# Partial results of the expert products: a running sum for product 7 alone, sum S1 on VectorE, scaling on ScalarE, and an in-SBUF finish in the last expert

## The chip, the cores and the metric

One core of one Trainium2 chip runs the whole program in one launch. The metric is the device time of that core in microseconds (us), the median of several executions. Of the core's engines TensorE (PE in the rows, its weight loads PEld) multiplies matrices, VectorE (DVE) and ScalarE (ACT) do elementwise work and are the ones that read the matmul results in PSUM, GpSimd (POOL) does elementwise work on SBUF and issues the transfers that add while they move data, and SyncE (SP) issues plain transfers.

## The reference

Attention with bucketed keys, then one gated block (`a * b @ w3 @ w_out`), then four experts. The change lies in the four experts only:

```python
def _moe2_ref(x, domain_probs, w1, w2):          # x [1536, 512], w1 [4, 512, 1024], w2 [4, 1024, 512]
    p = domain_probs / (domain_probs.sum(-1, keepdims=True) + 1e-09)
    out = np.zeros((N, D), dtype=np.float32)
    for e in range(E):                            # E = 4
        h = np.maximum(x @ w1[e], 0.0)
        out += p[:, e:e + 1] * (h @ w2[e])
    return out
```

## The kernel before

All matrices are float32. A float32 operand is split into a high part (rounded to the fast matmul type, done by ScalarE) and a low part (the rest, done by VectorE), and each product is three matmuls: high-high, high-low, low-high. Every operand of TensorE therefore needs one ScalarE and one VectorE instruction first.

**The two stages of an expert.** Both products of an expert use Strassen's scheme in Winograd's form: seven half-size products P1 to P7 in place of eight. The first stage (`fp_products`) makes the hidden activations, kept in eight pairs of SBUF rows (`kept`). The second stage multiplies them with `w2`. It runs the products in the order P1, P4, P6, P7, P5, P2, P3. Each product has four slices s = 0 to 3 (`slice_mm`): a slice's left operand is split into `hl` by `split_a` (ScalarE high part at line 1062, VectorE low part at line 185, or line 1064 for P2, which is negated), and then TensorE runs 18 matmuls. There are three `hl` buffers, so the split of a slice can start when the slice three before it has been multiplied. The left operands of P6, P7, P5 and P3 are sums of hidden activations, S2 (for P6), S3 (P7), S1 (P5) and S4 (P3): before, S3 is made by GpSimd, S2 and S4 by VectorE (`combine`, line 1070), and S1 by a transfer that adds in SBUF, issued by GpSimd (`sums_d`, line 1197). The right operands (`ring`) are prepared by `prep_b` (ScalarE line 1223, VectorE line 185 or 1228).

**What becomes of a product.** P1, P6, P5 and P3 pile up in one group of three PSUM banks, and P4, P7, P2 in the other, P4, P7 and P2 each starting afresh. After every product `results` reads its three banks, k = 0 to 2 (each two tiles of 128 tokens by 256 columns). It scales them by the tokens' probabilities into one of four buffers `stage` (parts of `g`, two `gl` and `cbuf`) and adds this buffer to a running sum `held` in HBM. The output has four quadrants (token half c, column half h). P1 and P2 go to quadrant (0,0), P4 and P6 to (1,0), P5 to (1,1), P3 to (0,1), and P7 to both (1,0) and (1,1): it is written twice. In the first expert the first product of each quadrant is written plainly by SP (line 1321); all later ones are added by a transfer that GpSimd issues (line 1325). A scaling instruction waits until the transfers of the buffer's last use have landed.

**Limits on the transfers.** `queued` makes each adding transfer wait until the third-last one has landed, so three are in flight at most.

**The last expert.** P1, P4 and the (1,1) half of P7 still go through `held`. Each quadrant's finished sum is read back by SP (line 1288) before its last product and VectorE adds the scaled last product in SBUF (line 1294), then SP stores the output (line 1301).

**The order of the work.** Every instruction is entered with an engine, a model duration, its dependencies and a priority; a planner (`emit_all`) simulates the engines and writes out each engine's queue in the order that results. On the chip each engine works through its own queue strictly in that order.

Of the kernel before, what the change touches and what calls it, by code (L numbers as in the profile page):

```python
# [85 lines left out]
def tile_lsh_attention_moe(ctx, tc, qk, v, projc, w1, w2, w3T, w_out, dp, e1, e2, out):  # L86
# [579 lines left out]
    held = {(c, h, k): dram.tile([128, 512], F32, name=f"held{c}{h}{k}") for c in range(2) for h in range(2) for k in range(3)}  # L666
# [392 lines left out]
    def split_a(n, src, after, relu, T=None, sign=1.0):  # L1059
# [3 lines left out]
        if relu or sign < 0:  # L1063
            op(("gl", n), "DVE", 900, lambda: nc.vector.scalar_tensor_tensor(
                out=lo(), in0=src(), scalar=0.0 if relu else sign, in1=f(hi()), op0=ALU.max if relu else ALU.mult, op1=ALU.subtract), [("gh", n)], T)
        else:
            op(("gl", n), "DVE", 900, lambda: lo_of(lo(), src(), hi()), [("gh", n)], T)
# [101 lines left out]
    OUTS = {1: ((0, 0),), 4: ((1, 0),), 6: ((1, 0),), 2: ((0, 0),), 5: ((1, 1),), 7: ((1, 0), (1, 1)), 3: ((0, 1),)}  # L1169
    FIRST = {(0, 0): 1, (1, 0): 4, (1, 1): 7, (0, 1): 3}  # L1170
# [87 lines left out]
    LAST = {(0, 0): 2, (1, 0): 7, (1, 1): 5, (0, 1): 3}  # L1258
    ng = [0]
    stage_free = [x_in + y_in for _ in range(4)]  # L1260
    back, begun = [], []

    def results(e, p):
        T = clock[0] + 1.5 * Q
        c = OUTS[p][0][0]
        halves = [h for _, h in OUTS[p]]
        final = e == NE - 1
        ends = [h for h in halves if final and (LAST[c, h] == p or p == 6)]
        adds = [h for h in halves if h not in ends]
        if final and p == 6:  # L1270
            for i in range(4):
                back.append([lambda i=i: raws[i // 2][:, i % 2 * 512:(i % 2 + 1) * 512], raw_free[0] if i < 2 else [("td", e, 6, i - 2)]])
        if final and p == 7:
            for s in range(4):
# [127 lines left out]
```

## Time and profile before

| | |
|---|---|
| median of 3 executions | 972.46 us (971.6 to 973.52) |
| the profiled execution's own time | 969.86 us |
| its span, first to last instruction | 968.1 us |
| TensorE busy | 950.0 us, 98% |
| VectorE, ScalarE, GpSimd busy | 745.1, 595.2, 355.7 us |
| granted TensorE clock, mean | 0.999 of full speed |

The page divides the span into 40 slices with the busy share of each engine, follows the chain of work that ended last, and lists groups of instructions by line with what ended the idle time before them. TensorE counts as busy while matmuls are in its pipeline, so 98% leaves few microseconds in which it stood still; the list in order of time gives each of these with the instruction that released it, in square brackets.

### The profile page before, as it was taken

The numbers are of one execution on the slowest core, as the hardware profiler recorded it, in microseconds if no ns is written. First come the engines' busy times: TensorE is split into PE (matmuls) and PEld (weight loads), VectorE is DVE, ScalarE is ACT, GpSimd is POOL, SyncE is SP. The second block draws the span as 40 slices with busy tenths as digits, with TensorE's granted clock in tenths as the row PEclk, the third lists the DMA queues.
The fourth block names the chain that finished last, engine by engine and source line by source line (L and its number), as shares of the span: only waits on it lengthen the run. The fifth ranks groups of instructions, "written<-read, shape, count | busy, mean of one in ns | idle before, by whom it ended". The sixth has DMA issues, their size and how long they took to land.

```text
span 968.1 us, 16584 instructions
## 1 busy us (share of the span) xinstructions
PE 950.0 (98%) x6091; PEld 859.2 (89%) x6091; DVE 745.1 (77%) x1374; ACT 595.2 (61%) x1105; POOL 355.7 (37%) x409
## 2 busy tenths in 40 slices
PE   8999999999999999999999999999989999899998
PEld 6989899998888888888888999889988899888997
DVE  6999999999699974965786875678756687565777
ACT  5989999888634332434586664666546665365552
POOL 6898788886200000000044223232442424524130
PEclk9999999999999999999999999999999999999999
DMA  6754444330133431310311566103991139910286
GB/s 167 188 130 125 111 110 119 98 94 15 55 109 131 131 109 43 109 44 1 110 33 34 136 135 166 45 23 67 202 168 33 33 57 188 185 40 12 34 186 207
DMA packets 59826, 96.40 MB, mean 100 GB/s; under 512 B 7480, under 2 KB 30328, under 8 KB 59744
## 3 DMA queue, kind: packets, MB, share of 16 engines
q1 hardware_dynamic: 47360, 70.94, 24.5%
q0 software_dynamic: 12240, 24.38, 16.0%
q8 instruction: 48, 0.79, 0.3%
q14 instruction: 34, 0.28, 0.1%
q10 hardware_dynamic: 144, 0.01, 0.0%
HBM read 50.36 MB, written 24.38 MB: 77 GB/s over the span
## 4 chain that ended last, share of the span: by engine, by line
PE 78%; DVE 6%; DMA 6%; ACT 5%; issue 3%; POOL 2%; SPq 0%; DVEq 0%; ACTq 0%; POOLq 0%
PE u_ps L176 38%; PE o_ps L176 25%; PE s_ps L176 5%; PE pv_ps L176 4%; DMA held<-g 2%; DVE e L495 2%; PE t_ps L543 2%; PE t_y L176 2%; PE t_x L543 2%; ACT e L498 1%; DMA wraw<-held 1%; DVE etx L551 1%; ACT etx L549 1%; PE t_y L543 1%; DMA r<-in_qk 1%
## 5 line engine op out<-in xcount | busy, mean ns | idle before, releaser
L176 PE MATMUL o_ps<-ring,hl 128*128 128x256 f32 x1008 | 124.6, 284 | 5.1 <-DVE hl L185 3.3
L176 PEld LDWEIGHTS o_ps<-ring,hl 128*128 128x128 f32 x1008 | 122.3, 192 | 6.5 <-DVE hl L185 4.1
L176 PE MATMUL u_ps<-ring,hl 128*128 128x256 f32 x1008 | 124.2, 283 | 2.1 <-DVE hl L185 1.3
L176 PEld LDWEIGHTS u_ps<-ring,hl 128*128 128x128 f32 x1008 | 122.3, 192 | 3.1 <-DVE hl L185 1.7
L907 POOL TENSOR_TENSOR ro<-ro 128x256 f32<-128x256 f32 x32 | 28.5, 891 | 255.3 <-PE o_ps L176 232.2
L498 ACT ACTIVATE e<-e,sm 128x768 f32<-128x768 f32 x96 | 89.3, 931 | 7.2 <-DVE e L495 6.3
L495 DVE TENSOR_SCALAR_CACHE_REDUCE e<-s_ps 128x768 f32<-128x768 f32 x96 | 89.9, 948 | 2.3 <-PE t_ps L543 1.2
L176 PE MATMUL u_ps<-xh,slot 128*128 128x512 f32 (+1 forms) x384 | 79.3, 363 | 0.0
L176 PEld LDWEIGHTS u_ps<-xh,slot 128*128 128x128 f32 x384 | 66.0, 189 | 11.6
L185 DVE TENSOR_TENSOR hl<-xa,hl 128x768 fp32r<-128x768 f32 (+1 forms) x60 | 54.1, 908 | 26.7 <-ACT hl L182 16.1
L508 POOL TENSOR_SCALAR e<-e,sm 128x768 f32<-128x768 f32 x72 | 67.1, 939 | 11.6 <-DVE sm L513 6.2
L176 PE MATMUL pv_ps<-etx,vv 128*128 128x256 f32 x384 | 58.2, 290 | 0.1
L1062 ACT ACTIVATE hl<-xa 128x768 fp32r<-128x768 f32 x56 | 46.5, 839 | 16.4 <-PE u_ps L176 5.9
L1325 POOL DMA_DIRECT2D held<-gl x34 | 30.6, 928 | 68.8 <-ACT gl L1312 28.1
L176 PE MATMUL s_ps<-ka,hh 128*128 128x512 f32 x192 | 52.7, 356 | 2.7 <-DVE e L495 1.8
L176 PE MATMUL u_ps<-xh,slotl 128*128 128x512 f32 (+1 forms) x264 | 54.4, 351 | 0.0
L176 PEld LDWEIGHTS pv_ps<-etx,vv 128*128 128x128 f32 x384 | 49.8, 189 | 1.9 <-DVE xa L571 0.8
L176 PE MATMUL u_ps<-xh,slotm 128*128 128x512 f32 x216 | 49.9, 389 | 0.0
L176 PE MATMUL s_ps<-kb,ll 76*128 76x512 f32 x192 | 49.6, 340 | 0.3 <-DMA kb<-bt 0.2
L176 PEld LDWEIGHTS u_ps<-xh,slotl 128*128 128x128 f32 x264 | 43.4, 189 | 6.8
L176 PEld LDWEIGHTS u_ps<-xh,slotm 128*128 128x128 f32 x216 | 40.5, 188 | 8.4
L551 DVE TENSOR_TENSOR etx<-t_x,etx 128x1024 fp32r<-128x1024 f32 x34 | 41.5, 1220 | 6.4 <-ACT etx L549 6.2
(244 smaller groups left out, 2298.0 us busy)
## 6 DMA issues: line engine op xcount, KB each, us to landing
held<-gl POOLq DMA_DIRECT2D x34, 256.0 KB, 5.2
wraw<-in_w SPq DMA_DIRECT2D x16, 512.0 KB
wraw<-in_w3T SPq DMA_DIRECT2D x16, 512.0 KB
wraw<-in_e SPq DMA_DIRECT2D x32, 256.0 KB
ro<-in_e SPq DMA_DIRECT2D x32, 256.0 KB
r<-in_qk SPq DMA_DIRECT2D x15, 384.0 KB
held<-cbuf POOLq DMA_DIRECT2D x18, 256.0 KB, 5.8
held<-g POOLq DMA_DIRECT2D x17, 256.0 KB, 5.8
```

The source lines that it names most:

```text
L176: nc.tensor.matmul(out=o, lhsT=l, rhs=r, start=start, stop=stop, skip_group_check=chained)
L185: nc.vector.tensor_tensor(out=dst, in0=ps, in1=f(hi), op=ALU.subtract)
L495: op(("mx", u, t), "DVE", 873, lambda ps=ps, m=m, e=e: nc.vector.tensor_scalar(out=cols(e), in0=row(ps), scalar1=THR, scalar2=None, op0=AL ...
L498: op(("ex", u, t), "ACT", 921, lambda e=e, m=m, rs=rs: nc.scalar.activation(out=e, in_=e, func=AF.Exp, scale=-1.0, bias=m, accum_out=rs), ...
L508: return "POOL", 872, lambda: nc.gpsimd.tensor_scalar(out=e, in0=e, scalar1=r[:, t:t + 1], scalar2=1.0, op0=ALU.mult, op1=ALU.mult)
L543: nc.tensor.transpose(out=ps[:, k, t * 128:(t + 1) * 128], in_=e_t[2 * (u % ER) + t][:, kt * 128:(kt + 1) * 128], identity=ident)
L549: op(("hi", n), "ACT", 480 if w == 2 else 907, lambda ps=ps_of, et=et_of: nc.scalar.activation(out=et()[:, 0], in_=ps(), func=AF.Copy), [( ...
L551: op(("lo", n), "DVE", 602 if w == 2 else 1136, lambda ps=ps_of, et=et_of: nc.vector.tensor_tensor(out=et()[:, 1], in0=ps(), in1=f(et()[:, ...
L907: op(("t", e, fp, m), "POOL", 1050 if m == 2 else 840, lambda m=m, x=x, y=y: nc.gpsimd.tensor_tensor(out=b_sum(m, fp)(), in0=x(), in1=y(), ...
L1062: op(("gh", n), "ACT", 850, lambda: nc.scalar.activation(out=hi(), in_=src(), func=AF.Relu if relu else AF.Copy, scale=sign), after, T)
L1325: landed = queued(key, 4 + k + 3 * half, 4000, lambda n=n, h=half, k=k: nc.gpsimd.dma_start(out=held[c, h, k], in_=stage(n), accum_op=ALU. ...
```

## The change

All of it is in the second stage of the experts.

- The running sums are numbered `HOLD`: 0 for P1 and P2, 1 for P4 and P6, 2 for P7, 3 for P5, 4 for P3. P7 is added once, to a sum of its own, in place of twice. There are 21 results of an expert to move in place of 24.
- In experts 0 to 2, S1 is added by VectorE in place of a transfer. In the last expert S1 is a transfer still, and S4, VectorE's before, becomes one too.
- Both halves of a bank are scaled by ScalarE; before, the second half was VectorE's.
- In the last expert only P1 still goes to HBM. The sums 1, 2, 3, 0 and 4 are read back into SBUF when their buffers come free, P4, P6, P7, P5, P2 and P3 are added there by VectorE, and VectorE adds sum 2 to sums 1 and 3 (six adds of 128x512).
- Some model durations of the planner change (low part 900 to 930, S sums 900 to 950, scaling 380 to 420, transfers 4000 to 5000), and with them queue orders.

```diff
-    held = {(c, h, k): dram.tile([128, 512], F32, name=f"held{c}{h}{k}") for c in range(2) for h in range(2) for k in range(3)}
+    held = {(m, k): dram.tile([128, 512], F32, name=f"held{m}{k}") for m in range(5) for k in range(3)}
...
+    HOLD = {1: 0, 2: 0, 4: 1, 6: 1, 7: 2, 5: 3, 3: 4}
+    HALF = {2: 0, 7: 0, 5: 1, 3: 1}
...
+    def sum_by(e, m, s, dst, src, after, T):
+        if e == NE - 1:
+            keys[("s", e, m, s)] = keys[queued(("sq", e, m, s), 4 + s, 4500, lambda: nc.gpsimd.dma_start(
+                out=dst(), in_=src(), accum_op=ALU.add), after, T)]
+        else:
+            op(("s", e, m, s), "DVE", 950, lambda: combine(dst(), dst(), src(), ALU.add), after, T)
 
     def sums_d(e, s):
-        dst, src = stored(0, 0, s), stored(1, 1, s)
-        keys[("s", e, 1, s)] = keys[queued(("sq", e, 1, s), s, 4000, lambda: nc.gpsimd.dma_start(
-            out=dst(), in_=src(), accum_op=ALU.add), [("s", e, 2, s), ("gl", an[1, s])], clock[0])]
+        sum_by(e, 1, s, stored(0, 0, s), stored(1, 1, s), [("s", e, 2, s), ("gl", an[1, s])], clock[0] + 0.4 * Q)
 
     def sums_c(e, s):
-        dst, src = stored(0, 1, s), stored(1, 1, s)
-        op(("s", e, 4, s), "DVE", 900, lambda: combine(dst(), dst(), src(), ALU.add), [("s", e, 2, s), ("gl", an[2, s])], clock[0])
+        sum_by(e, 4, s, stored(0, 1, s), stored(1, 1, s), [("s", e, 2, s), ("gl", an[2, s])], clock[0])
...
+    def read_back(e, p, k, m, place, free_, T):
+        buf[m, k] = place, [("l3", m, k)]
+        op(("l3", m, k), "SP", 800, lambda: nc.sync.dma_start(out=place(), in_=held[m, k]), region[m, k] + free_, T - 10 * Q)
...
+                if p == 7:
+                    for m_ in (1, 3):
+                        x_, r_ = buf[m_, k]
+                        op(("as", m_, k), "DVE", 620, lambda o=o, x_=x_: combine(x_(), x_(), o(), ALU.add), got + r_, T + (5 if m_ == 1 else 1.5) * Q)
+                        buf[m_, k] = x_, [("as", m_, k)]
...
-                    if h == 0 or ends:
-                        op(got[h], "ACT", 380, lambda n=n, b=b, x=x, t=t0 + h: nc.scalar.activation(
-                            out=stage(n)[:, x], in_=psb(b)[:, x], func=AF.Copy, scale=prob[:, t, e:e + 1]), done + stage_free[n % 4], T)
-                    else:
-                        op(got[h], "DVE", 350, lambda n=n, b=b, x=x, t=t0 + h: nc.vector.tensor_scalar(
-                            out=stage(n)[:, x], in0=psb(b)[:, x], scalar1=prob[:, t, e:e + 1], scalar2=None, op0=ALU.mult), done + stage_free[n % 4], T)
+                op(got[h], "ACT", 420, lambda n=n, b=b, x=x, t=t0 + h: nc.scalar.activation(
+                    out=stage(n)[:, x], in_=psb(b)[:, x], func=AF.Copy, scale=prob[:, t, e:e + 1]), done + stage_free[n % 4], T)
...
+            if e == 0 and p not in (2, 6):
+                op(key, "SP", 800, lambda n=n, k=k: nc.sync.dma_start(out=held[m, k], in_=stage(n)), got, T)
+                op(key + ("on",), f"Q{k}", 2500, lambda: None, [key], T)
+            else:
+                queued(key, k, 5000, lambda n=n, k=k: nc.gpsimd.dma_start(out=held[m, k], in_=stage(n), accum_op=ALU.add), got + region[m, k], T)
```

VectorE's queue in expert 1, from P2's third slice to P3's last, before. `hl` rows at lines 1064 and 185 are low parts of P2's and P3's slices, line 1070 is S4, and line 1315 is scaling into a stage buffer.

```order
L1064 SCALAR_TENSOR_TENSOR hl_3014<-g_68,hl_3014 128x768
L1070 TENSOR_TENSOR g_68<-g_68,gl_3011 128x768
L1064 SCALAR_TENSOR_TENSOR hl_3012<-gl_3010,hl_3012 128x768
L1315 TENSOR_SCALAR cbuf<-o_ps_3032,prob 128x256
L1070 TENSOR_TENSOR gl_3010<-gl_3010,cbuf 128x768
L185 TENSOR_TENSOR hl_3013<-xa,hl_3013 128x768
L185 TENSOR_TENSOR hl_3014<-xa,hl_3014 128x768
L1315 TENSOR_SCALAR g_68<-u_ps_3026,prob 128x256
L1315 TENSOR_SCALAR gl_3010<-u_ps_3027,prob 128x256
L1315 TENSOR_SCALAR gl_3011<-u_ps_3028,prob 128x256
L185 TENSOR_TENSOR hl_3012<-g_68,hl_3012 128x768
L185 TENSOR_TENSOR hl_3013<-gl_3010,hl_3013 128x768
```

The same place now:

```order
L1064 SCALAR_TENSOR_TENSOR hl_3017<-g_68,hl_3017 128x768
L1070 TENSOR_TENSOR g_68<-g_68,gl_3014 128x768
L1064 SCALAR_TENSOR_TENSOR hl_3015<-gl_3013,hl_3015 128x768
L1070 TENSOR_TENSOR gl_3013<-gl_3013,cbuf 128x768
L185 TENSOR_TENSOR hl_3016<-xa,hl_3016 128x768
L185 TENSOR_TENSOR hl_3017<-xa,hl_3017 128x768
L185 TENSOR_TENSOR hl_3015<-g_68,hl_3015 128x768
L185 TENSOR_TENSOR hl_3016<-gl_3013,hl_3016 128x768
```

No scaling row is left between the low parts, so nothing in this stretch of VectorE's queue refers to a stage buffer or a PSUM bank.

ScalarE's queue in expert 1 where P1 is read out, before (line 1062 high parts of P4's and P6's slices, line 1223 right operands, line 1312 scaling):

```order
L1062 ACTIVATE hl_3013<-gl_3011 128x768
L1223 ACTIVATE ring<-wraw_70 128x2x256
L1312 ACTIVATE gl_3010<-o_ps_3030,prob 128x256
L1312 ACTIVATE gl_3011<-o_ps_3031,prob 128x256
L1062 ACTIVATE hl_3014<-cbuf 128x768
L1312 ACTIVATE cbuf<-o_ps_3032,prob 128x256
L1223 ACTIVATE ring<-wraw_70 128x2x256
L1062 ACTIVATE hl_3012<-xa 128x768
```

and now:

```order
L1062 ACTIVATE hl_3016<-gl_3014 128x768
L1227 ACTIVATE ring<-wraw_70 128x2x256
L1326 ACTIVATE gl_3013<-o_ps_3033,prob 128x256 x2
L1062 ACTIVATE hl_3017<-cbuf 128x768
L1326 ACTIVATE gl_3014<-o_ps_3034,prob 128x256 x2
L1326 ACTIVATE cbuf<-o_ps_3035,prob 128x256
L1227 ACTIVATE ring<-wraw_70 128x2x256
L1326 ACTIVATE cbuf<-o_ps_3035,prob 128x256
L1062 ACTIVATE hl_3015<-xa 128x768
```

Six scaling instructions stand where there were three, spread around the same high parts.

GpSimd's transfers in the last expert, now the whole list (before there were four S1 transfers and nine to `held`, three of P4 ahead of S1 and three of P7 behind it):

```order
L1334 DMA held_139<-cbuf 128x512
L1334 DMA held_140<-g_68 128x512
L1334 DMA held_141<-gl_3013 128x512
L1197 DMA xa<-xa 128x768 x2
L1197 DMA g_68<-gl_3014 128x768
L1197 DMA gl_3013<-cbuf 128x768
L1197 DMA xa<-xa 128x768 x2
L1197 DMA g_68<-gl_3014 128x768
L1197 DMA gl_3013<-cbuf 128x768
```

The three transfers of P1 come first, then S1, then S4, which needs P2's low parts.

## Rows read from the trace of the kernel before

**Rows 1.** TensorE in order of time, expert 0: start, length, instructions, [idle before, releaser].
```profile
535.16 8.80 PE L176 MATMUL u_ps<-ring,hl 128*128 128x256 f32 x72
...
595.63 4.37 PE L176 MATMUL o_ps<-xh,slot 128*128 128x256 f32 x24
```

**Rows 2.** The same view, expert 1, P1's start to the next expert's start.
```profile
654.58 8.80 PE L176 MATMUL o_ps<-ring,hl 128*128 128x256 f32 x72
...
707.65 0.50 PE L176 MATMUL o_ps<-ring,hl 128*128 128x256 f32 x2 [0.62 <-ACT hl L1062]
709.17 4.58 PE L176 MATMUL o_ps<-ring,hl 128*128 128x256 f32 x36 [1.02 <-DVE hl L185]
...
718.61 4.37 PE L176 MATMUL u_ps<-xh,slot 128*128 128x256 f32 x24
```

**Rows 3.** The same view, expert 2's first product and the next expert's start.
```profile
777.57 8.80 PE L176 MATMUL u_ps<-ring,hl 128*128 128x256 f32 x72
...
841.31 4.37 PE L176 MATMUL o_ps<-xh,slot 128*128 128x256 f32 x24
```

**Rows 4.** The same view, last expert: P1, inside P5, inside P2, P3.
```profile
900.31 8.80 PE L176 MATMUL o_ps<-ring,hl 128*128 128x256 f32 x72
...
936.87 8.65 PE L176 MATMUL o_ps<-ring,hl 128*128 128x256 f32 x70 [1.60 <-DVE hl L185]
...
952.80 2.17 PE L176 MATMUL u_ps<-ring,hl 128*128 128x256 f32 x16 [0.56 <-DVE hl L1064]
954.80 9.07 PE L176 MATMUL o_ps<-ring,hl 128*128 128x256 f32 x72
```

**Rows 5.** VectorE in order of time, expert 1, P5 and P3.
```profile
691.83 0.48 DVE L1315 TENSOR_SCALAR cbuf<-u_ps,prob 128x256 f32<-128x256 f32 x1 [2.55 <-DMA held<-cbuf]
...
713.03 0.48 DVE L1315 TENSOR_SCALAR gl<-u_ps,prob 128x256 f32<-128x256 f32 x1 [1.49 <-DMA held<-gl]
713.43 0.95 DVE L185 TENSOR_TENSOR hl<-g,hl 128x768 fp32r<-128x768 f32 x1
```

**Rows 6.** ScalarE in order of time, expert 1, inside P2.
```profile
706.39 0.47 ACT L1312 ACTIVATE cbuf<-o_ps,prob 128x256 f32<-128x256 f32 x1 [4.24 <-DMA held<-cbuf]
```

**Rows 7.** Transfers by queue, 535 to 596 us (expert 0): packets, MB, share of 16 engines.
```profile
q0 software_dynamic: 2304, 4.72, 47.7%
q1 hardware_dynamic: 2809, 4.80, 21.9%
```

**Rows 8.** The same view, 654 to 719 us (expert 1).
```profile
q0 software_dynamic: 3557, 7.02, 69.5%
q1 hardware_dynamic: 1617, 2.54, 11.8%
```

**Rows 9.** The same view, 900 to 968 us, and S1's transfers: count, KB, us to landing.
```profile
q0 software_dynamic: 1872, 3.93, 35.9%
q1 hardware_dynamic: 4992, 6.29, 26.9%
...
xa<-xa POOLq DMA_DIRECT2D x2, 384.0 KB, 7.4
...
g<-gl POOLq DMA_DIRECT2D x1, 384.0 KB, 9.2
```

**Rows 10.** The line of the adding transfers: issue ns min/median/max, and us to landing.
```profile
L1325 POOL DMA_DIRECT2D held<-gl x34: 865/880/1225, 563.2 to 942.0; - x34
...
DMA to landing us min/median/max: 3.9/5.7/9.2
```

**Rows 11.** Busy time by engine in expert 1's second stage (columns: PE, PEld, DVE, ACT, POOL).
```profile
654.60:718.60 64.00, 61.48 (x505) 60.66 (x504) 47.63 (x71) 34.73 (x57) 23.82 (x26) 1.00 0.82 147
```

**Rows 12.** Groups by line and shape, 476 to 968 us: busy us, mean ns | idle before.
```profile
L1070 DVE TENSOR_TENSOR xa<-xa 128x768 f32<-128x768 f32 x16 | 15.2, 953 | 0.2
...
L1062 ACT ACTIVATE hl<-xa 128x768 fp32r<-128x768 f32 x56 | 46.5, 839 | 16.4 <-PE u_ps L176 5.9 <-PE o_ps L176 5.4 <-ACT hl L1062 2.9
...
L1223 ACT ACTIVATE ring<-ro 128x512 fp32r<-128x512 f32 x32 | 20.0, 624 | 15.3 <-PE u_ps L176 8.4 <-PE o_ps L176 6.9
```

More of the change, by code (lines that the diff above doesn't have):

```diff
@@ L1256, in slice_mm, with scaled_sum, half_raw, row_of @@
         clock[0] += 0.82 * Q
-    LAST = {(0, 0): 2, (1, 0): 7, (1, 1): 5, (0, 1): 3}
     ng = [0]
     stage_free = [x_in + y_in for _ in range(4)]
-    back, begun = [], []
+    buf = {}
+    def scaled_sum(o, ps, t, e):
+        nc.vector.scalar_tensor_tensor(out=o, in0=ps, scalar=prob[:, t, e:e + 1], in1=o, op0=ALU.mult, op1=ALU.add)
+    def read_back(e, p, k, m, place, free_, T):
+        buf[m, k] = place, [("l3", m, k)]
+        op(("l3", m, k), "SP", 800, lambda: nc.sync.dma_start(out=place(), in_=held[m, k]), region[m, k] + free_, T - 10 * Q)
+    def half_raw(i):
+        return (lambda: raws[i // 2][:, i % 2 * 512:(i % 2 + 1) * 512]), (raw_free[0] if i < 2 else [("td", NE - 1, 6, i - 2)])
+    def row_of(s):
+        return (lambda: kept(1, 2 * s)[:, 0:512]), [("gl", an[7, s])]
     def results(e, p):
         T = clock[0] + 1.5 * Q
[L1265 to L1274, printed above, removed]
-                back.append([lambda s=s: kept(1, 2 * s)[:, 0:512], [("gl", an[7, s])]])
+        m = HOLD[p]
+        c = 0 if p in (1, 2, 3) else 1
         for k, b in enumerate(banks_of(e, p)):
@@ L1279, in results @@
             done = [("X", e, p, 3)]
-            read = []
-            for half in ends:
-                w = slice(half * 256, (half + 1) * 256)
-                if p == 7:
-                    buf, loaded = begun.pop(0)
-                else:
-                    buf, free_ = back.pop(0)
-                    loaded = [("l3", p, k)]
-                    op(("l3", p, k), "SP", 800, lambda buf=buf, h=half, k=k: nc.sync.dma_start(out=buf(), in_=held[c, h, k]),
-                       region[c, half, k] + free_, T - 10 * Q)
+            if e == NE - 1 and p != 1:
+                if p == 4:
+                    read_back(e, p, k, 1, *(half_raw(k) if k < 2 else ((lambda n=ng[0]: stage(n)), stage_free[ng[0] % 4])), T)
+                elif p == 7:
+                    n = (ng[0] + 1 + k) % 4
+                    if k < 2:
+                        read_back(e, p, k, 2, *half_raw(2 + k), T)
+                        read_back(e, p, k, 3, lambda n=n: stage(n), stage_free[n], T)
+                    else:
+                        read_back(e, p, k, 2, lambda n=n: stage(n), stage_free[n], T)
+                        read_back(e, p, k, 3, *row_of(0), T)
+                elif p == 2:
+                    read_back(e, p, k, 0, *row_of(1 + k), T)
+                elif p == 3:
+                    read_back(e, p, k, 4, buf[2, k][0], [("as", 1, k), ("as", 3, k)], T)
+                o, ready = buf[m, k]
                 got = []
@@ new lines, in results @@
+                if p not in (4, 6):
+                    half = HALF[p]
+                    o, got = buf[1 if p == 7 else m, k]
+                    op(("st", p, k), "SP", 800, lambda rows=rows, o=o, w=slice(half * 256, (half + 1) * 256): nc.sync.dma_start(
+                        out=rows[:, :, w], in_=o().rearrange("p (r c) -> p r c", r=2)), got, T)
+                continue
+            n = ng[0]
+            ng[0] += 1
+            got = [("sg", e, p, k, h) for h in range(2)]
+            for h in range(2):
+                x = slice(h * 256, (h + 1) * 256)
+                op(got[h], "ACT", 420, lambda n=n, b=b, x=x, t=t0 + h: nc.scalar.activation(
+                    out=stage(n)[:, x], in_=psb(b)[:, x], func=AF.Copy, scale=prob[:, t, e:e + 1]), done + stage_free[n % 4], T)
```

46 lines of the change are left out of this document (10 added, 36 removed).

## The prediction

> **What bounds the kernel now.** I read the page first: TensorE is busy 98% of the span, so no engine beside it can shorten the run except by removing moments in which TensorE stands still. The chain that ended last names where these are: from the first expert on it runs along TensorE, and leaves it only in the second stages of experts 1, 2 and 3, for adding transfers, VectorE and reads of `held`. So I went to TensorE's list in order of time.
>
> In expert 0 the second stage has no stall: seven products from 535.16 to 595.63, 60.47 us, 8.64 us each [rows 1]. This is the pace to compare with. Expert 1 takes 718.61 - 654.58 = 64.03 us, so 3.56 us are lost; the list shows P3's start waiting for a high part and then for low parts [rows 2]. Expert 2 takes 841.31 - 777.57 = 63.74 us, 3.27 us lost [rows 3]. In expert 3, P1 to P2 take 954.80 - 900.31 = 54.49 us where six products at 8.64 need 51.83: 2.66 us lost, most of it in P5 and P2 [rows 4]. Together **9.49 us** are lost between expert 1 and P3 of the last. Everything else (attention, the gated block, the first stages, the tail) the change leaves alone; its queue orders differ only from the end of expert 0's first stage on.
>
> Why do they stall? The lists of the two helpers in expert 1 answer it. VectorE stood 2.55 us at a scaling row in P5 until a stage buffer's transfer landed, and 1.49 us at another in P3; the low part of P3's third slice, which TensorE was waiting for, came directly behind it [rows 5]. ScalarE stood 4.24 us at a scaling row in P2 [rows 6]. So the buffers come back late, and because queues are in order, a scaling row that waits holds up the splits behind it. And why late? In expert 1 the adding transfers (q0) took 69.5% of the sixteen engines in a window of 65 us, 45.2 us, and plain transfers 11.8%, 7.7 us [rows 8]. Nearly all of that falls after P1's end at about 663 us, so about 53 us of transfers in 55 us: the engines are full. Expert 0, which did not stall, had 47.7% and 21.9% of 61 us, 42.5 us [rows 7].
>
> **The change, part by part.**
>
> *Fewer adding transfers.* Expert 1 loses three `held` transfers (P7's second writing) of 256 KB and four S1 transfers of 384 KB: 24 x 0.262 + 4 x 0.393 = 7.86 MB become 21 x 0.262 = 5.50 MB. At 45.2 us for 7.02 MB [rows 8], 6.4 us per MB, that is 35.4 us; with the 7.7 us of plain transfers 43.1 us in the same 55. This is almost exactly expert 0's load, at which nothing stalled. At three transfers per product and a median landing of 5.7 us [rows 10] a buffer has ample time: from a product's end ScalarE does a split (0.84), a cast (0.62) and two scalings (0.47 each) [rows 6, 12], so block 0 leaves at about 2.4 us and its transfer lands near 8.4 us; the next product wants that buffer for its block 1, after one split more, at 8.64 + 2.4 + 0.84 = 11.9 us. Margin 3.5 us at the median landing, 0 at the longest, 9.2 us [rows 10]. I take experts 1 and 2 as gaining all they lost but 0.3 us each, since plain loads of the next expert's weights still crowd P6 to P5: (3.56 - 0.3) + (3.27 - 0.3) = **6.2 us**. Bounds: 0 and 6.83.
>
> *Scaling all on ScalarE.* VectorE loses 21 rows of 0.48 us [rows 5] per expert, 10.1 us; ScalarE gains 21 x 0.47 = 9.9 us [rows 6], which takes it from 34.73 us [rows 11] to 44.6 of 60.5. What counts is the order: in the 4.3 us after a product's end, between its own high parts, ScalarE now does two splits, two casts and six scalings, 1.7 + 1.2 + 2.8 = 5.7 us by full durations, so the next high part starts about 1.4 us late. A split may start two slices (4.3 us) before it is multiplied and needs 0.84 + 0.95 us plus handovers, which leaves some 2 us. Cost 0; the cover is those 2 us, and a late landing eats them.
>
> *S1 on VectorE.* Four adds of 0.95 us [rows 12] per expert, 3.8 us, in P4 and P6, against six scaling rows (2.9 us) that left the same two products. VectorE works 47.63 of 64 us [rows 11]; after the change about 41. It waits for nothing outside, as its inputs come earlier on its own queue. Cost 0.
>
> *The last expert.* P4's three transfers no longer stand ahead of S1's four, and by the rule of three in flight S1 waits for P1's transfers alone, the last of which lands, by the median, near 908.95 + 4.8 + 5.7 = 919.5 us, one and a half products before P5 needs S1; S1 was late before (7.4 and 9.2 us to land [rows 9]), and P5 waited. The sums P6 and P2 need are read one or two products earlier, so VectorE no longer stands before them. That frees the 2.66 us. Against it, S4 is now four 384 KB transfers between P2's low parts and P3. The fourth can be issued when P2's last low part is done, about 4.3 us after P2's start, lands between 3.9 and 9.2 us later, so 8.2 to 13.5 us after P2's start, and P3's fourth slice must be split from 8.64 + 3 x 2.16 - 2.1 = 13.0 us on. Mostly in time; I set 0.5 us for it. VectorE's 12 new rows (six adds, P4's six) replace four S4 adds and six scalings, even. Transfer load is equal: three `held` and eight SBUF transfers are again 3.93 MB [rows 9]. Gain 2.66 - 0.5 = **2.2 us**; bounds 2.66 and, with rival A's 3.8 us, -1.1.
>
> **Sum.** 6.2 + 2.2 = 8.4 us. The profiled execution, 969.86 us, would become 961.5. It lies 2.6 us under the median of the runs, 972.46, and against that median the time is **964.0 us**.
>
> **The rivals.**
>
> *A: buffers or S4 still late, half the gain.* For: transfers from SP and GpSimd share the engines, and S1 took 7.4 and 9.2 us to land when reads ran beside it [rows 9]. If S4's transfers take 9.2 us, the first lands at 7.6 us after P2's start (P2's first split may begin 4.3 us before it and takes 1.8, on a VectorE that is busy with sums just then, so I put the issue 1.6 us before it); the fourth must wait for it (three in flight) and lands at 16.8, 3.8 us too late for P3. If in addition P7, P5, P2 and P3 of experts 1 and 2 lose 0.3 us each, 2.4 us in all instead of 0.6, the gain is 6.83 - 2.4 + 2.66 - 3.8 = 3.3: 969.2 us; with S4 alone late, 967.4. Against: expert 0's load did not stall.
>
> *A2: GpSimd cannot issue while VectorE adds.* S4's four issues would run amid VectorE's busiest stretch. The longest issue in the trace is 1.225 us against a median of 0.88 [rows 10], so eight issues in line could lose 8 x 0.35 = 2.8 us, all before P3: 964.0 + 2.8 = 966.8. The Trainium skill ("SBUF — State Buffer", Who interferes with whom) says that VectorE in a two-port mode, or with two SBUF inputs against a GpSimd operation that reads SBUF, locks the port GpSimd shares, that descriptors then can't be written, and gives 620 ns alone against 3100 overlapped. By these figures each issue would lose 2.5 us, 10 us for four. The trace bears out a seventh of that at most.
>
> *B: nothing measurable.* The waits may come from the length of a landing and not from load, and move whole from VectorE to ScalarE, where every scaling now stands. For: ScalarE's 4.24 us [rows 6] were such a wait. Against: the landing that ended it came behind P7's six and S1's four transfers, which go. Time 970.5 to 974.4.
>
> *C: slower, ScalarE as gate.* Both halves of every block now wait on the one engine that starts every split. If landings passed 9.2 + 2 us in each product behind P1, every further microsecond would stop TensorE: to lose the 8.4 us and 1.9 more over 12 products of experts 1 and 2 takes 0.86 us each, a landing of about 12 us; at 12.3 us the time would be 964.0 + 12 x 1.1 = 977. No transfer to `held` took over 9.2.
>
> **How the numbers follow.** A change of under 0.2%, 1.9 us, can hardly be told from none. Forecast (961.8 to 966.3): 0.60. A and A2 (to 970.5): 0.20, of which A2 0.03. B: 0.10. C: 0.10. All but B and C are faster: 0.80, same 0.10, slower 0.10. The low end is the whole 9.49 us gained, 963.0, less 1.2 us for the spread of the runs; the high end is A's: 961.8 to 970.5.
>
> **What would show it.** Right: TensorE's seven products of experts 1 and 2 in about 60.8 us each, no scaling row on VectorE, ScalarE's waits for `held` under 1 us each, q0's share near 54% of expert 1's window, P5 of the last expert starting with no wait. Wrong: idle before a TensorE row released by ScalarE's `hl` behind a scaling row that waited for `held` (A, C); P3 of the last expert waiting for low parts whose S4 transfer landed late (A, A2); the first stage of the following expert starting as late as before although transfers got fewer (B).

## The result, and the profile after

The changed kernel takes **960.2 us** (median of 4 runs, 959.0 to 960.83), the kernel before, now with 4 runs, 972.03 (969.02 to 973.52): a ratio of 0.988, 95% interval 0.9855 to 0.9907. It is faster, as forecast, but lies 1.6 us under the low end of the range. The profiled execution of after took 960.83 us, that of before 969.86: 9.03 us between the two.

First the list that the prediction was made from: TensorE in order of time, experts 1 to 3, to be held against [rows 2 to 4].

```profile
655.06 8.80 PE L176 MATMUL o_ps<-ring,hl 128*128 128x256 f32 x72
...
715.54 4.37 PE L176 MATMUL u_ps<-xh,slot 128*128 128x256 f32 x24
...
774.50 8.80 PE L176 MATMUL u_ps<-ring,hl 128*128 128x256 f32 x72
...
834.97 4.37 PE L176 MATMUL o_ps<-xh,slot 128*128 128x256 f32 x24
...
893.93 8.80 PE L176 MATMUL o_ps<-ring,hl 128*128 128x256 f32 x72
...
928.48 8.80 PE L176 MATMUL o_ps<-ring,hl 128*128 128x256 f32 x72
...
945.76 8.80 PE L176 MATMUL o_ps<-ring,hl 128*128 128x256 f32 x72
```

Each second stage takes 60.47 to 60.48 us, the pace of [rows 1], and the last expert's six products 945.76 - 893.93 = 51.83. No row has a wait in brackets: all the stalls of [rows 2 to 4] are gone. So the saving must be looked for in what the helpers wait for. The line of the scaling instructions on ScalarE, what ended its idle time (us, times):

```profile
L1326 ACT ACTIVATE gl<-u_ps,prob x34: 453/468/501, 547.3 to 838.3; 128x256 f32<-128x256 f32 x34
...
its engine sat idle before it (us, times) until:
  PE u_ps L176: 7.1, 2
  PE o_ps L176: 3.6, 1
```

They waited only for products, three times; for a transfer never, where ScalarE and VectorE had stood 4.24, 2.55 and 1.49 us [rows 5, 6]. The transfers by queue, 654 to 715 us, and the adding transfers' line:

```profile
q0 software_dynamic: 2510, 4.59, 53.3%
q1 hardware_dynamic: 1696, 2.62, 13.7%
...
L1334 POOL DMA_DIRECT2D held<-gl x25: 851/872/1058, 564.1 to 908.5; - x25
```

Adding transfers have 53.3% of the sixteen engines in place of 69.5 [rows 8] (67.2 in this same window, shown below); the prediction said near 54. The busy time in the same stage, to be held against [rows 11]:

```profile
655.10:715.50 60.40, 60.40 (x505) 60.40 (x504) 43.22 (x55) 41.39 (x76) 17.57 (x19) 1.00 0.67 118
```

ScalarE works 41.39 us where the prediction's sum said 44.6, VectorE 43.22 where it said about 41; both leave room. All this fits the prediction's account, load taken away and buffers back in time. The experiments show that this is one of two ways in which these stalls can go.

### The profile page after: what moved, and what is told of

Same layout as the page of the kernel before. It is cut to its first block, busy times and chain, and to the rows that moved or that the text cites. A ratio compares the mean times of both kernels' runs of the same rounds, so it can differ in the third digit from the quotient of the medians.

```text
span 958.9 us, 16468 instructions
## 1 busy us (share of the span) xinstructions
PE 947.4 (99%) x6091; PEld 859.1 (90%) x6091; DVE 731.9 (76%) x1325; ACT 614.2 (64%) x1162; POOL 331.8 (35%) x383
## 4 chain that ended last, share of the span: by engine, by line
PE 89%; DVE 6%; ACT 3%; issue 1%; DMA 0%; SPq 0%; DVEq 0%; ACTq 0%
PE u_ps L176 43%; PE o_ps L176 29%; PE s_ps L176 6%; PE pv_ps L176 5%; DVE e L495 2%; PE t_y L176 2%; PE t_ps L543 2%; PE t_x L543 2%; DVE etx L551 1%; ACT e L498 1%; PE t_y L543 1%; DVE ety L551 1%; ACT etx L549 1%; DMA r<-in_qk 0%; ACT ety L549 0%
## 5 line engine op out<-in xcount | busy, mean ns | idle before, releaser
L1334 POOL DMA_DIRECT2D held<-gl x25 | 22.2, 899 | 69.3 <-ACT gl L1326 67.9
```

The lines of the kernel that those rows point to most:

```text
L1334: queued(key, k, 5000, lambda n=n, k=k: nc.gpsimd.dma_start(out=held[m, k], in_=stage(n), accum_op=ALU.add), got + region[m, k], T)
```

## The experiments

Losses are counted on TensorE: in experts 1 and 2 what a period, P1's start to the next expert's P1, has over the 119.44 us of after (774.50 - 655.06); in the last expert what P1 to P3 takes over 51.83. "Rest" is the profiled execution's time less both. Ratios are to runs of before on the same chip.

| kernel | median us | ratio, 95% interval | profiled | experts 1, 2 | last | rest |
|---|---|---|---|---|---|---|
| before, first profile | 972.03 | 1 | 969.86 | 3.55 + 3.30 | 2.66 | 960.4 |
| b_rep1 | 970.76 | 0.9996 to 1.0015 | 973.36 | 4.62 + 3.69 | 5.01 | 960.0 |
| b_rep2 | 971.92 (one run) | | 971.92 | 3.89 + 3.54 | 4.37 | 960.1 |
| after | 960.2 | 0.9855 to 0.9907 | 960.83 | 0 | 0 | 960.8 |
| b_s1 | 965.66 | 0.9936 to 0.9963 | 965.66 | 1.86 + 1.49 | 2.60 | 959.7 |
| b_act | 973.59 | 1.0005 to 1.0033 | 973.87 | 4.23 + 3.76 | 5.70 | 960.2 |
| a_split | 959.46 | 0.9862 to 0.9900 | 959.76 | 0 + 0.20 | 0 | 959.6 |
| a_s1 | 959.8 | 0.9865 to 0.9903 | 959.95 | 0.67 + 0 | 0 | 959.3 |
| a_p7 | 960.19 | 0.9869 to 0.9905 | 958.79 | 0 | 0 | 958.8 |
| a_load | 961.74 | 0.9882 to 0.9934 | 962.50 | 1.63 + 0.92 | 0 | 960.0 |
| a_both | 960.63 | 0.9862 to 0.9904 | 961.39 | 0 | 0 | 961.4 |
| a_both_s1 | 960.21 | 0.9860 to 0.9899 | 959.52 | 0.15 + 0 | 0 | 959.4 |
| a_dur | 959.59 | 0.9852 to 0.9897 | 959.26 | 0 | 0 | 959.3 |
| a_heavy_lane | 966.92 | 0.9951 to 0.9977 | 966.78 | 4.54 + 2.62 | 0 | 959.6 |
| b_5000 | 967.33 | 0.9947 to 0.9974 | 967.63 | 2.37 + 0.88 | 3.69 | 960.7 |
| b_act_dur | 967.5 | 0.9955 to 0.9982 | 968.69 | 0.01 + 0.88 | 7.97 | 959.8 |
| b_s1l | 969.01 | 0.9969 to 0.9993 | 968.94 | 3.40 + 4.35 | 0.74 | 960.5 |
| b_s1all_dur | 963.17 | 0.9908 to 0.9947 | 962.71 | 0 | 0 (2.75 in P3) | 960.0 |
| a_p4 | 970.84 | 0.9979 to 1.0005 | 969.36 | 0 | 10.24 | 959.1 |
| a_p4_s1 | 962.13 | 0.9892 to 0.9929 | 961.82 | 0 | 1.23 | 960.6 |

b_ kernels start from before, a_ kernels from after. (a_both_s1's last period and its last expert show no stall either.) Each loss is that of one profiled execution, the median that of several.

### Where the missing 2.6 us were: before again, twice

No edit. b_rep1: 

> The kernel before, once more, for a second profile and more run times. Theory O1 (the runs of the kernel before differ in how long TensorE is stalled in the experts' second stages): the profiled time less the stalls counted in TensorE's list (second stages of experts 1 to 3 over 60.47 us each, and over 51.83 us for six products of the last) stays near 969.86 - 9.49 = 960.4 us, within 0.7, whatever the time. Rival O2 (most runs carry about 2.6 us somewhere else, and the changed kernel loses them by chance): the stalls stay near 9.5 us and the time less the stalls moves.

b_rep2: 

> The kernel before, a third profile. O1: time less stalls again 960.4 us within 0.7. O2: stalls again near 9.5 us, time less stalls elsewhere, up to 963.

TensorE in P5 of b_rep1's last expert:

```profile
939.95 10.15 PE L176 MATMUL o_ps<-ring,hl 128*128 128x256 f32 x70 [3.26 <-DVE hl L185]
```

The wait that was 1.60 us in [rows 4] is 3.26 us here, 2.62 in b_rep2. The time without the losses is 960.0 to 960.4 in all three executions, while the losses run from 9.5 to 13.3. So the profiled executions of before differ by the size of these very stalls, and the prediction's had the smallest of the three. The median that it was held against, 972.46, was in turn a high one: it came from three runs, and in later sets of 11 to 33 runs before has medians of 970.25 to 971.46.

### Load, or the place of the scaling rows: both alone fail

b_s1 takes S1 off the transfers in experts 0 to 2 of before; b_act gives all scaling to ScalarE, in before; a_split gives the second halves back to VectorE, in after:

```diff
 b_s1, sums_d:
+        if e < NE - 1:
+            op(("s", e, 1, s), "DVE", 900, lambda: combine(dst(), dst(), src(), ALU.add), [("s", e, 2, s), ("gl", an[1, s])], clock[0] + 0.4 * Q)
+            return
 b_act, results:
-                    if h == 0 or ends:
+                    if h < 2:
 a_split, results (for h == 1):
-                op(got[h], "ACT", 420, ...
+                op(got[h], "DVE", 350, lambda n=n, b=b, x=x, t=t0 + h: nc.vector.tensor_scalar(...
```

b_s1: 

> The kernel before with one part of the change: S1 added by VectorE in experts 0 to 2. Theory T (the adding transfers fill the transfer engines, stage buffers come back late, and a scaling row that waits for one holds the splits behind it): transfers of expert 1 fall from about 53 us to 24 x 0.262 MB x 6.4 + 7.7 = 48 us in 55, so of the 6.83 us lost in experts 1 and 2 at most 3 stay; the last expert's 2.66 us stay; 4 to 6 us faster than before. Rival V (the place of the scaling rows in VectorE's queue makes the stalls, whatever the transfer load): VectorE keeps its scaling rows and gains four adds, so no gain, or slower by up to 4 us.

b_act: 

> The kernel before with one other part: both halves of every block scaled by ScalarE. T: the transfer load is as before, so the waits move to ScalarE's queue and the time stays within 2 us of before. V: VectorE never waits for a stage buffer, so most of the 6.83 us of experts 1 and 2 go, 5 to 7 us faster.

a_split: 

> The changed kernel with the scaling shared again, second halves by VectorE. T: at the lighter transfer load no buffer is late, so no stall: within 1 us of the changed kernel (960.2). V: the scaling rows on VectorE bring back most of 6.83 us: 965 to 967.

All three went as the load theory says: less load takes half of the loss in experts 1 and 2 (3.35 us stay, a little over the 3 expected), and moving the scaling rows between the engines saves nothing. In b_act the waits stay and change their releaser, here in P2 of expert 1, where TensorE waits for ScalarE's high part:

```profile
706.01 0.50 PE L176 MATMUL u_ps<-ring,hl 128*128 128x256 f32 x2 [1.48 <-ACT hl L1062]
```

So far the prediction's account stands. Then the load was put back into after:

```diff
 a_s1, sum_by (S1 is four transfers in every expert):
-        if e == NE - 1:
+        if e == NE - 1 or m == 1:
 a_p7, a_load, results (P7's blocks go a second time to sums that nobody reads; a_load adds S2 likewise):
+            if p == 7:
+                more = ("dz", e, k)
...
+                    queued(more, k, 5000, lambda n=n, k=k: nc.gpsimd.dma_start(out=again[k], in_=stage(n), accum_op=ALU.add), got + region["again", k], T)
...
 a_both, results (P7 of experts 1 and 2 goes to P4/P6's and to P5's sum, as in before):
+            elif p == 7:
...
+                for m_ in (1, 3):
+                    queued(key + (m_,), k, 5000, lambda ...: nc.gpsimd.dma_start(out=held[m_, k], in_=stage(n), accum_op=ALU.add), got + region[m_, k], T)
...
```

a_both_s1 is a_both with a_s1's edit.

a_s1: 

> The changed kernel with S1 as adding transfers in all experts. T: expert 1's transfers are 21 x 0.262 + 4 x 0.393 MB = 7.07 MB, 45.5 us, and 7.7 us of plain ones: again 53 us in 55. Stalls come back, now released by ScalarE behind scaling rows that wait for held: 3 to 7 us slower than the changed kernel. V: no scaling row is on VectorE, so no stall, within 1 us of it.

a_p7: 

> The changed kernel with P7's stage buffers transferred twice in experts 0 to 2, the second time to a sum that nobody reads (24 results moved per expert). T: 40.5 + 7.7 = 48 us of transfers in 55; P7's buffers come back later; 0 to 3 us slower than the changed kernel. V: within 1 us of it.

a_load: 

> The changed kernel with the whole transfer load of before put back in experts 0 to 2 as transfers that nobody reads: P7's buffers twice, and S2's four results of 384 KB added to HBM. Scaling stays on ScalarE and S1 on VectorE. T: 53 us of transfers in 55 again, stalls of 4 to 8 us, released by ScalarE. V: the load does not matter while VectorE has no scaling row, within 1 us of the changed kernel.

a_both: 

> The same without S1's transfers (S1 by VectorE): P7's blocks of experts 1 and 2 go to P4/P6's sums and to P5's. L: about half of the 6 to 8 us, since the chain of landings is there and a third of the extra bytes: 962 to 965 us. N and D: 960 to 961.

a_both_s1: 

> The changed kernel with the kernel of before's transfers back where they were: P7's blocks of experts 1 and 2 go to P4/P6's sums and to P5's (expert 0's stay in a sum of their own, so that the results are the reference's), and S1 is four adding transfers in every expert; scaling stays on ScalarE, with the new planner durations. Theory L (P7's second transfer on a sum that P6 has just been adding to and that P5 adds to next, a chain of landings, and S1's transfers between them, make the stage buffers late): experts 1 and 2 lose what the kernel of before with all scaling on ScalarE lost there, 6 to 8 us, the last expert nothing: 966 to 968.5 us. Rival N (the bytes matter, not the sums they go to): as with the same bytes to sums nobody waits for, 2 to 3 us lost: 961.5 to 963. Rival D (the planner's durations make the difference, not the transfers): 960 to 961.

Here the load theory fails. a_s1, a_p7 and a_both stay within 1 us of after, and a_load loses 2.55 us where T asked for 4 to 8. a_both_s1 moves by the adding queue in expert 1 what before does, to the same sums and, but for two exchanged rows, in the same order on GpSimd: 6.32 MB and 69.2% of the engines between 654 and 715 us, against 6.41 MB and 67.2% of before in the same window:

```profile
q0 software_dynamic: 3181, 6.32, 69.2%
```

```profile
q0 software_dynamic: 3227, 6.41, 67.2%
```

(the first is a_both_s1, the second before). It loses 0.15 us where b_act, with the same transfers and the same scaling engine, loses 8. Theory L fell with theory T; N's 2 to 3 us, which a_load showed, did not come either. Its time is the one that rival D named.

### What is left: the order of the queues

In experts 1 and 2, what is left between b_act and a_both_s1 is what the planner is told, and the orders that it makes of it: durations, a priority of S1's, and lanes. (A lane is one of the planner's model queues; the transfers of one lane land one after the other. Before has ten, after has seven.) ScalarE in order of time, expert 1, P5's readout. First a_heavy_lane, which is a_both_s1 with before's durations and lanes and has b_act's order in this stretch:

```profile
699.20 0.84 ACT L1326 ACTIVATE gl<-o_ps,prob 128x256 f32<-128x256 f32 x2 [1.13 <-DMA held<-gl]
703.55 0.84 ACT L1326 ACTIVATE gl<-o_ps,prob 128x256 f32<-128x256 f32 x2 [3.51 <-DMA held<-gl]
704.28 0.84 ACT L1062 ACTIVATE hl<-gl 128x768 fp32r<-128x768 f32 x1
707.89 0.84 ACT L1326 ACTIVATE cbuf<-o_ps,prob 128x256 f32<-128x256 f32 x2 [2.78 <-DMA held<-cbuf]
708.62 1.57 ACT L1062 ACTIVATE hl<-xa 128x768 fp32r<-128x768 f32 x2
```

Then a_both_s1, told 5000 ns for a transfer to a held sum instead of 4000, on after's lanes:

```profile
698.29 0.84 ACT L1326 ACTIVATE gl<-o_ps,prob 128x256 f32<-128x256 f32 x2 [0.43 <-DMA held<-gl]
699.90 0.84 ACT L1062 ACTIVATE hl<-gl 128x768 fp32r<-128x768 f32 x1 [0.76 <-PE u_ps L176]
702.11 0.85 ACT L1062 ACTIVATE hl<-xa 128x768 fp32r<-128x768 f32 x1 [1.36 <-PE u_ps L176]
703.37 0.84 ACT L1326 ACTIVATE gl<-o_ps,prob 128x256 f32<-128x256 f32 x2 [0.42 <-DMA held<-gl]
```

The second block's scaling starts at about the same moment, 703.55 and 703.37: its buffer comes back no earlier. But in the first order the high part of `gl` stands behind it, those of `xa` behind the third block too, and they start at 704.28 and 708.62; in the second `gl` and the first of `xa` stand ahead and start at 699.90 and 702.11. TensorE shows the price, a_heavy_lane in P2 and P3:

```profile
705.17 0.51 PE L176 MATMUL u_ps<-ring,hl 128*128 128x256 f32 x2 [1.21 <-ACT hl L1062]
...
709.52 0.51 PE L176 MATMUL o_ps<-ring,hl 128*128 128x256 f32 x2 [1.19 <-ACT hl L1062]
```

And a_dur, after with before's numbers, so the first order at the light load:

```profile
697.62 1.55 ACT L1326 ACTIVATE gl<-o_ps,prob 128x256 f32<-128x256 f32 x4
699.05 0.86 ACT L1062 ACTIVATE hl<-gl 128x768 fp32r<-128x768 f32 x1
```

Four scaling rows in a line without a wait: there the buffers are free in time, and the order does no harm. The changed kernel itself has this first order here:

```profile
699.09 1.55 ACT L1326 ACTIVATE gl<-o_ps,prob 128x256 f32<-128x256 f32 x4
700.51 0.86 ACT L1062 ACTIVATE hl<-gl 128x768 fp32r<-128x768 f32 x1
```

So at this place after owes its pace to the light load; from the same numbers the planner made the second order only where it had the old load to plan for (a_both_s1).

```diff
 a_dur: after with 900, 900, 380, 4000, 4000 for 930, 950, 420, 5000, 4500
 a_heavy_lane: a_both_s1 with the same, and before's ten model lanes
 b_5000, results of before:
-                        landed = queued(key, 4 + k + 3 * half, 4000, ...
+                        landed = queued(key, 4 + k + 3 * half, 5000, ...
 b_act_dur: b_act with 930, 950, 420, 5000, 4500
 b_s1all_dur: before with S1 by VectorE in all experts (late, clock[0] + 0.4 * Q) and 930, 950, 420, 5000
```

a_dur: 

> The changed kernel with the planner durations of before (low parts 900, sums 900, scaling on ScalarE 380, transfers 4000), nothing else. L and N: no difference, 959.5 to 961 us. D: the queues are ordered as badly as before and some of the 9 to 13 us come back: 963 to 970.

a_heavy_lane: 

> The changed kernel with before's transfers (P7's blocks of experts 1 and 2 added to P4/P6's and P5's sums, S1 as four transfers in every expert) and before's planner numbers (transfers 4000 ns on ten lanes, low parts and sums 900, scaling 380): the load of before with ScalarE's queue in the order of before, in which P5's first three scaling rows, and two of its next block, stand ahead of a split. Theory O (load and order together: a scaling row that waits for a transfer holds the splits queued behind it): experts 1 and 2 lose 7 to 8.5 us, as in the kernel of before with all scaling on ScalarE, the last expert nothing: 966.5 to 969 us. Rival N (something else of the changed kernel, not the order, made the load harmless): 960 to 961.5.

b_5000: 

> The kernel of before with one number changed, which no instruction reads: the planner is told 5000 instead of 4000 ns for a transfer to a held sum. Work, engines and bytes are before's; the order of the queues near P5, P2 and P3 of experts 1 and 2 changes. O: most of the 6.8 to 8.4 us that before lost in experts 1 and 2 is gained, the last expert's 2.7 to 5 us stay: 963 to 966.5 us. N, and the theory that the load alone makes the stalls: 970 to 972.

b_act_dur: 

> The kernel of before with all scaling on ScalarE, which lost 8.05 us in experts 1 and 2, and with all planner durations of the changed kernel (5000, 4500, 950, 930, 420). O: those 8 us are gained but for 1 or 2, the last expert's stalls stay: 964.5 to 968 us. N: 972 to 974.

b_s1all_dur: 

> The kernel of before with S1 added by VectorE in all four experts, and the planner's numbers of the changed kernel (5000, 950, 930, 420). P7 still adds its blocks to P4/P6's and P5's sums, and P6's and P7's sums of the last expert are read late, both as before. Theory O with H (order and load in experts 1 and 2, S1's transfers in the last): experts 1 and 2 lose under 1.5 us together, the last under 1: 960.5 to 963 us. Rival P (P7's own sum and the early reads are needed for half of the gain or more): 965 to 967.5.

The four corners at one scaling engine, by what the planner is told: old numbers and old load lose 8.0 (b_act) and 7.2 us (a_heavy_lane), old numbers and light load 0 (a_dur), new numbers and old load 0.15 (a_both_s1) and 0.9 (b_act_dur), new numbers and light load 0 (after). D, by which the numbers alone would bring some of the stalls back in a_dur (963 to 970), fell there: 959.59. In these corners a stall needs both, an old load and an order with splits behind late scaling rows; a_load, below, is the exception. In the last expert the new numbers alone do not help: b_act_dur loses 7.97 us there, b_act 5.70 (one execution each). b_5000 is before with one number changed that no instruction reads; on ScalarE it moves three high parts per expert ahead of one or two scaling rows, in expert 1 for instance P3's last one, in P2's readout:

```diff
 L1312 ACTIVATE g_68<-u_ps_3026,prob 128x256
+L1062 ACTIVATE hl_3013<-gl_3010 128x768
 L1312 ACTIVATE gl_3010<-u_ps_3027,prob 128x256
 L1312 ACTIVATE gl_3011<-u_ps_3028,prob 128x256
-L1062 ACTIVATE hl_3013<-gl_3010 128x768
```

Of the 6.85 to 8.3 us that before loses in experts 1 and 2, 3.25 stay; that is about half and not O's "most", and its median, 967.33, is above the 963 to 966.5 expected. By the medians on one chip it gains 2.9 us (970.25 to 967.33). P5's readout shows why half stays: its second block still stands ahead of the high part of `gl`, which starts at 702.48 behind it, and TensorE waits 1.02 us in P2:

```profile
702.11 0.47 ACT L1312 ACTIVATE gl<-o_ps,prob 128x256 f32<-128x256 f32 x1 [3.77 <-DMA held<-gl]
```

What the sharing of the scaling between the engines adds was not separated from the other numbers here. b_s1all_dur loses nothing in experts 1 and 2, without P7's own sum. Rival P fell, but the time is 0.2 us over what was expected: P3 of the last expert waits 2.75 us for a low part behind VectorE's rows at 943.82 and 945.48, which stood 2.46 and 0.79 us for reads of `held`:

```profile
943.82 0.88 DVE L1293 SCALAR_TENSOR_TENSOR wraw<-o_ps,prob,wraw 128x256 f32<-128x256 f32 x2 [2.46 <-DMA wraw<-held]
945.48 1.66 DVE L1293 SCALAR_TENSOR_TENSOR xa<-o_ps,prob,xa 128x256 f32<-128x256 f32 x4 [0.79 <-DMA xa<-held]
947.06 1.81 DVE L185 TENSOR_TENSOR hl<-xa,hl 128x768 fp32r<-128x768 f32 x2
```

### The last expert

```diff
 a_p4, results: P4 goes to its sum by transfer, which is read back at P6
-            if e == NE - 1 and p != 1:
-                if p == 4:
+            if e == NE - 1 and p not in (1, 4):
+                if p == 6:
 a_p4_s1: the same, and S1 of the last expert by VectorE
 b_s1l: before, S1 of the last expert alone by VectorE
```

a_p4: 

> The changed kernel with the last expert's P4 as before: its blocks go by adding transfer to P4/P6's sum, and the sum is read back at P6 instead of at P4. Theory H (in the last expert P4's three transfers ahead of S1's made P5 late): S1's transfers land later again, P5 waits 2.5 to 5 us: 962.5 to 965.5 us, with TensorE's wait in P5 before a low part. Rival E (the six reads at P6 and P7, issued late, held VectorE in front of the low parts, and P4's transfers matter little): under 1 us in P5: 959.5 to 961.

b_s1l: 

> The kernel of before with S1 of the last expert alone added by VectorE instead of four transfers. Theory H (S1's transfers land late behind P4's and hold P5): the last expert's 2.7 to 5 us go, experts 1 and 2 keep 6.8 to 8.4: 966.5 to 968.5 us. Rival E (the reads of the sum that P6 needs are issued late, since P4's transfers must land first, and VectorE stands at P6's adding rows ahead of P5's splits): VectorE still waits 3 us or more for the reads, and 2 us or more of the stalls stay: 969 to 971.5.

a_p4_s1: 

> The changed kernel with P4 of the last expert as before (added to P4/P6's sum, which is read back at P6), and S1 of the last expert by VectorE instead of four transfers. H: the 10.2 us that the same without the second edit lost go, but for 1 or 2: 960 to 962.5 us, although VectorE still waits for the reads at P6. E (the late reads): 4 us or more stay: 964 to 968.

GpSimd's issues of S1 in a_p4, start and wait:

```profile
915.33 0.87 POOL L1334 DMA_DIRECT2D held<-g  x1 [0.81 <-ACT g L1326]
916.45 0.87 POOL L1197 DMA_DIRECT2D xa<-xa  x1 [0.25 <-issue]
...
925.55 0.88 POOL L1197 DMA_DIRECT2D gl<-cbuf  x1 [1.72 <-issue]
```

In after, GpSimd issued them at:

```profile
909.87 0.87 POOL L1197 DMA_DIRECT2D xa<-xa  x1 [0.52 <-DVE hl L185]
...
918.08 0.87 POOL L1197 DMA_DIRECT2D gl<-cbuf  x1 [1.41 <-DVE hl L185]
```

Counted from P1's start (892.14 and 893.93), the first goes out 24.3 us in instead of 15.9, the last 33.4 instead of 24.2; P5 starts after four products, 34.56. In a_p4 ScalarE then waits for them (2.12 and 1.80 us at P5's first two high parts; the second is shown), and VectorE, at the row that adds P6, for a read, with P7's last low part (`hl<-cbuf`) behind it:

```profile
927.97 0.84 ACT L1062 ACTIVATE hl<-xa 128x768 fp32r<-128x768 f32 x1 [1.80 <-DMA xa<-xa]
```

```profile
927.42 0.88 DVE L1267 SCALAR_TENSOR_TENSOR wraw<-o_ps,prob,wraw 128x256 f32<-128x256 f32 x2 [6.85 <-DMA wraw<-held]
928.21 0.95 DVE L185 TENSOR_TENSOR hl<-cbuf,hl 128x768 fp32r<-128x768 f32 x1
```

TensorE stands for low parts twice, in P7 and in P5:

```profile
929.22 3.59 PE L176 MATMUL u_ps<-ring,hl 128*128 128x256 f32 x16 [4.28 <-DVE hl L185]
...
935.57 10.15 PE L176 MATMUL o_ps<-ring,hl 128*128 128x256 f32 x70 [2.44 <-DVE hl L185]
```

By the starts of the products (918.05, 932.60, 945.57) P7 takes 14.55 us and P5 12.97 instead of 8.64: 5.9 us are lost in P7 and 4.3 in P5. Both low parts stood behind adding rows that waited for reads, which is E's path; but the loss, 10.24 us, is more than either forecast. The chain of work that ended last (start, length) shows what P5's low part waited for in a_p4, the landing of P4's third transfer and then the read of its sum:

```profile
915.33 7.31 DMA held<-g
...
922.69 11.07 DMA gl<-held
```

In a_p4_s1 the read on that chain takes 6.23 us:

```profile
919.88 6.23 DMA wraw<-held
```

The two runs without S1's transfers lose 1.23 (a_p4_s1) and 0.74 us (b_s1l), though VectorE still waits 2.6 and 4.1 us for reads there. So H and E are no alternatives: with S1's transfers beside them the reads take longer, and the adding rows that wait for the reads hold the low parts. S1's transfers alone cost nothing (after has them, and TensorE no wait), P4's transfers and the late reads without S1's cost 1.23, all together 10.24. Whether P4's transfers or the later reading is what after gains by, and why before, with the same seven transfers, loses only 2.66 to 5.01 us, no run separated. Before's wait in P5 [rows 4] has the same form, VectorE in order of time:

```profile
934.47 0.48 DVE L1294 SCALAR_TENSOR_TENSOR wraw<-o_ps,prob,wraw 128x256 f32<-128x256 f32 x1 [1.98 <-DMA wraw<-held]
...
935.87 1.82 DVE L185 TENSOR_TENSOR hl<-xa,hl 128x768 fp32r<-128x768 f32 x2
```

b_s1l's median, 969.01, is 0.5 us above H's range and at the low end of E's; by its stalls it meets H's forecast for the last expert (0.74 left) and E's for the reads (4.1 us of waiting).

## Why the prediction was right and wrong

- **What bounds, and which stalls go: right.** TensorE's losses [rows 2 to 4] were all that could be saved and all went; no scaling row on VectorE, no wait of ScalarE for `held`, q0 at 53.3%.
- **The step that failed** is in the sum: "It lies 2.6 us under the median of the runs, 972.46, and against that median the time is 964.0 us". It carried the distance between before's profiled run and before's median, which was that of three runs, over to the changed kernel, as if it were a constant. The two executions of b_rep1 and b_rep2 show what makes the time vary: larger sizes of the same stalls (13.3 and 11.8 us for 9.5), with the rest at 960.0 to 960.4. A change that removes the stalls removes their spread too; the profiled run less its losses, 969.86 - 9.49 = 960.4, was the whole answer, and the low end, 963.0 less 1.2, carried the same 2.6. That is 2.6 of the 3.8 us missed.
- **A term mis-sized:** 0.3 + 0.3 us left in experts 1 and 2 and 0.5 for S4, 1.1 us. All measured 0. The 6.2 us are 6.83, the 2.2 are 2.66. S4's transfers were issued 935.77 to 941.60, the last 4.5 us after P2's start as estimated, and TensorE waited for none in P3. It was close: ScalarE's last high part there stood 1.87 us for the fourth.

```profile
948.56 0.85 ACT L1062 ACTIVATE hl<-gl 128x768 fp32r<-128x768 f32 x1 [1.87 <-DMA gl<-cbuf]
```

- **"The engines are full", so the buffers are late, so it stalls: right for the change as made, and incomplete.** At the light load neither set of numbers stalls (a_dur and after). But at the old load the order that the new numbers make brings experts 1 and 2 to 0.15 us (a_both_s1), with the engines as full as before. The list of the change names the planner's durations; the prediction gave them no term, and in before one of them is worth 3.6 to 5.1 us there (b_5000, by the profiled executions). The lighter load was enough for the stalls to go; that full transfer engines must stall TensorE is what a_both_s1 refutes. (In the margin sum, 2.4 + 5.7 is 8.1 and not 8.4; the margin is 0.3 us larger, which changes nothing.)
- **Scaling on ScalarE at cost 0, S1 on VectorE at cost 0: right.** a_split, with the halves shared again, is within the interval of after; b_act shows no gain from the move itself. S1 on VectorE is what takes half of the loss (b_s1).
- **The last expert: right place, and both of its reasons act together.** The prediction named S1's late transfers and the sums read late. The wait that ended last was VectorE's for a read, ahead of P5's low parts, and S1's transfers made the reads late (b_s1l, a_p4, a_p4_s1). Late reads without S1's transfers cost less: 1.23 us in a_p4_s1, 2.75 in P3 of b_s1all_dur.
- **Rivals.** A and C did not happen: no landing over 8.1 us on the line of the transfers to `held`, 8.8 at most for S1 and S4, and no wait of TensorE. A2 neither: S4's issues took 0.87 to 0.89 us while VectorE ran instructions with two SBUF inputs. Two of those rows, of VectorE in order of time, and the issues beside them:

```profile
938.14 0.94 DVE L1064 SCALAR_TENSOR_TENSOR hl<-g,hl 128x768 fp32r<-128x768 f32 x1
...
941.51 0.68 DVE L1070 TENSOR_TENSOR wraw<-wraw,wraw 128x512 f32<-128x512 f32 x1
```

```profile
937.84 0.89 POOL L1197 DMA_DIRECT2D xa<-xa  x1 [1.21 <-DVE hl L1064]
...
941.60 0.87 POOL L1197 DMA_DIRECT2D gl<-cbuf  x1 [1.24 <-DVE xa L1267]
```

The Trainium skill ("SBUF — State Buffer", Who interferes with whom) also says, further on in that section, that an add with two inputs takes only the reading side of the shared port, and infers that writing descriptors needs the other side; the trace agrees with that note (0.87 us beside an add, against 0.88 median before), and the 2.5 us per issue weighed in the prediction do not apply to these adds. The Trainium skill has the 620 and 3100 ns in another section of the same title (A bandwidth-pool intuition that's wrong), for a DMA beside a copy by VectorE.
- **Rival B,** that waits would move whole to ScalarE, is what b_act did (8.0 us, with waits released by ScalarE's `hl`). It named a true mechanism; after escapes it through the light load.

What stays open: what P7's own sum alone would have brought (a_p7's second transfer cost nothing, but with the new numbers), and why a_load, with the new numbers, still lost 2.55 us where a_both_s1 at about the same load lost 0.15. Its stall has the known form: in expert 1 the scaling rows of P7's second and third block stood 1.31 and 2.10 us for transfers, with P2's first two splits behind them, where in a_both_s1 the same rows stood 0.16 us and none. Why the buffers come back later there is not shown; the first-stage products are interleaved differently too, which no run separated.

## What to carry to other kernels

Where a run's time varies from one execution to the next, look whether the stalls that a change removes vary with it: then forecast from a profiled run less its stalls, not from the median less the gain. In a kernel whose queues are in order, a late buffer costs only what stands behind the row that waits for it; moving independent work ahead of that row can be worth as much as making the buffer come earlier (here by what the planner is told; 5000 ns instead of 4000 for a transfer that takes 5 to 6 us gained 2.9 us by itself). And to see which of two causes acts, put each back alone: here, a_load apart, each was all but harmless without the other.

## What the runs showed that was not expected

The adding queue at 66 to 69% of the sixteen engines does not by itself delay TensorE: a_both_s1 ran so at full pace, with landings of 4.8 to 5.5 us (medians by tile, 654 to 715 us) against 5.0 to 5.5 in a_heavy_lane, which lost 4.5 us in that expert. And P4's three transfers of 256 KB, put back ahead of S1's four of 384 KB with their sum read later, cost 10.24 us in the last expert (a_p4), 1.23 without S1's four (a_p4_s1), and S1's four alone nothing (after): a_p4's median, 970.84, is before's again (970.75 on the same chip).
